# Output products of linear attention as 64-row tiles, the heads of either parity in a bank of their own, two chunks at once

## The chip, the cores and the metric

One core of one Trainium2 chip. Times are device microseconds of one execution, medians of several; a lower time is better. The engines are named as in the profile: PE is TensorE's matmul row, PEld its weight loads, DVE VectorE, ACT ScalarE, POOL GpSimd, SP the engine that issues most transfers.

## The reference

```python
# q, k, v: (batch 8, heads 8, seq 576, dim 64); all float32
kv  = einsum('bhsd,bhse->bhde', k, v)              # one 64x64 state per head
out = einsum('bhsd,bhde->bhse', q, kv)             # the output products: what the change is about
out = out / sqrt(mean(out**2, -1) + 1e-6) * g_norm
x   = out.transpose(0, 2, 1, 3).reshape(4608, 512)
xn  = x / sqrt(mean(x**2, -1) + 1e-6) * rms_g
y   = (silu(xn @ w_gate) * (xn @ w_val)) @ w_out   # 512 -> 1536 -> 512
```

## The kernel before

Everything is bfloat16 on TensorE, with float32 sums in PSUM. Of each batch's 576 tokens, 512 are worked on in a stage of their own (four chunks of 128 tokens); the 64 tokens left over of all eight batches make a ninth stage ("tail"). A stage has twelve units of gate and value products (`up`, eight matmuls of 512 columns each) and then four blocks of down products. While the units of batch n run, the attention of batch n+1 is slipped in between them: the state products of k and v, then the output products of a chunk after each of four units. Batches 0 and 1 are done by other code.

Two heads sit together in the 128 partitions of `qt`. Their states stand as two 64x64 blocks on the diagonal of a 128x128 block of `kv_all`, whose other two blocks are zero, so that one full-size product gives both heads, and half of its multiplications are with zeros.

```python
# four PSUM pools of two banks each (gate, value, down, attention)
outa_pool = pool("outa", 4)
gps_pool = pool("gps", 2, space=PS)
vps_pool = pool("vps", 2, space=PS)
ops_pool = pool("ops", 2, space=PS)
att_pool = pool("att", 2, space=PS)

# class Att (batches 2 to 7 and the tail)
def o_products(self, c, ps):
    for j in range(NS):                               # NS = 4 pairs of heads
        cols = ps[:, 2 * j : 2 * j + 2, :]
        if self.tail:
            ...                                       # 128-row, 64-column tiles, one per batch of two
        else:
            PE.matmul(
                cols, lhsT=self.qt[:, j, 128 * c : 128 * c + 128], rhs=kv_all[:, self.n, j, :],
                start=(j == 0), stop=(j == NS - 1),
            )

def o(self, c):
    ps = att_pool.tile([128, H, D], FP32, name="att_ps")
    self.o_products(c, ps)
    self.sq[c] = sq_pool.tile([128, 2, H, D], BF16, name="sq")
    SC.activation(out=self.sq[c][:, 0], in_=ps, func=ACT.Square)
    self.outa[c] = outa_pool.tile([128, H, D], BF16, name="outa")
    SC.copy(out=self.outa[c], in_=ps)

def sums(self, c):                                    # VectorE: the sums of squares of a chunk
    ...

# the schedule: what follows which unit of batch n
    kv0, os = (2, (4, 5, 7, 8)) if n == 1 else (0, (2, 3, 5, 6))
    if not a.tail:
        steps[kv0] += [lambda a=a: a.kv_products((0, 1))]
        steps[kv0 + 1] += [lambda a=a: a.kv_products((2, 3)), a.kv_copy]
    for c, u in enumerate(os):
        steps[u].append(lambda a=a, c=c: a.o(c))
        steps[u + 1].append(lambda a=a, c=c: a.sums(c))
    late = 2 * int(n == 1)
    steps[8 + late] += [a.head]
    steps[9 + late] += [a.guess, a.root]
    ...                                               # then scale and transpose each chunk
```

## Time and profile before

| | before |
|---|---|
| median (first three runs) | 324.66 us (324.35 to 336.14) |
| profiled run, span, granted clock | 324.46 us, 322.7 us, 1.0 |
| twelve units with attention of batches 3 to 7 | 22.73 us |
| twelve units of the last stage, nothing slipped in | 20.73 us |
| four down blocks | 10.36 us |

The page of the kernel before. In the upper part are busy time, share of the span and number of instructions; in the groups, count, then busy time and mean ns of one, then the idle time ahead of them and what ended it.

```profile
span 322.7 us, 5143 instructions
PE 316.0 (98%) x1925; PEld 156.5 (49%) x1925; DVE 181.5 (56%) x373; ACT 178.3 (55%) x318; POOL 20.3 (6%) x42
...
L352 ACT ACTIVATE sq<-att_ps 128x512 bf16<-128x512 f32 x28 | 16.7, 597 | 13.1 <-PE att_ps L343 8.7
L354 ACT CAST outa<-att_ps 128x512 bf16<-128x512 f32 x28 | 16.2, 579 | 0.0
L343 PEld LDWEIGHTS <-qt 128*128 128x128 bf16 x96 | 7.4, 98 | 5.7
L343 PE MATMUL att_ps<-kv_all,qt 128*128 128x128 bf16 x96 | 9.3, 219 | 0.0
```

PE has no idle time worth the name; no other engine passes 56%. The 96 output products look like 9.3 us of PE, but matmuls overlap in their pipeline and a duration of 219 ns is a latency. What a product costs is the distance from its start to the next start.

The stretches of stages, kernel before: busy time of each engine within each stretch, the number of instructions, the granted clock.

```profile
core 0: us, PE busy (x) PEld busy (x) DVE busy (x) ACT busy (x) POOL busy (x), PEclk, DMA share, GB/s
...
122.30:145.03 22.73, 22.73 (x133) 11.42 (x132) 15.65 (x32) 13.02 (x25) 0.00 (x0) 1.00 0.70 186
```

PE fills the whole stretch and the others have a third of it to spare, so what is slipped in between the units lengthens the stage by its PE time and by nothing else. Over the 20.73 us of the last stage it is 2.0 us: 20 state products and 16 output products of 128 columns at 56 ns.

The timeline of PE around two chunks, kernel before (start, time until the last of the merged instructions ends, what they are, how many):

```profile
160.82 1.03 PE L472 MATMUL v_ps<-xnt,wv_sb 128*128 128x512 bf16 x4
161.69 0.39 PE L343 MATMUL att_ps<-kv_all,qt 128*128 128x128 bf16 x4
161.91 1.03 PE L472 MATMUL g_ps<-xnt,wg_sb 128*128 128x512 bf16 x4
162.78 1.03 PE L472 MATMUL v_ps<-xnt,wv_sb 128*128 128x512 bf16 x4
163.64 0.39 PE L343 MATMUL att_ps<-kv_all,qt 128*128 128x128 bf16 x4
```

Four value products take 4 x 216 ns, 160.82 to 161.69. Four output products take 161.69 to 161.91: 0.22 us, 4 x 56 ns. Two chunks: 448 ns.

The kernel before holds smaller tiles already, and they show what going in and out of them costs. PE's timeline around the state products of batch 1 (64x64 tiles), and around the first chunk of the tail (128x64):

```profile
39.10 1.03 PE L472 MATMUL v_ps<-xnt,wv_sb 128*128 128x512 bf16 x4
40.06 1.32 PE L265 MATMUL att_ps<-vb,kb 64*64 64x64 bf16 x72
41.31 1.04 PE L516 MATMUL o_ps<-wo_sb,h_sb 128*128 128x512 bf16 x4
...
258.98 1.03 PE L472 MATMUL v_ps<-xnt,wv_sb 128*128 128x512 bf16 x4
259.94 0.41 PE L338 MATMUL att_ps<-kv_all,qt 128*64 128x128 bf16 x8
260.28 1.04 PE L472 MATMUL g_ps<-xnt,wg_sb 128*128 128x512 bf16 x4
```

From 258.98 to 259.94 is 0.96 us where 4 x 216 ns = 0.86 are due: the first tile comes 0.1 us late. Its eight products are four pairs that run side by side, 56 ns a pair, which would be 0.22 us; they take 0.34. So another 0.1 us is lost on the way out. PE counts as busy all the time, since the 379 ns of the matmul before cover the gap. What does show it is the weight loads: those of the same tiles have idle time ahead of them that is put down to "issue", that is, to nothing that the profile sees. From the view of that source line, kernel before:

```profile
L338 PEld LDWEIGHTS <-qt x32: 106/110/110, 259.9 to 268.3; 128*64 128x64 bf16 x32
...
its engine sat idle before it (us, times) until:
  issue: 1.7, 4
```

### The profile page before, as it was taken

Reading aid. Unit: us, or ns where it says so; the run is one execution under the profiler, and the core shown is the slowest. Engines: PE = TensorE matmul, PEld = TensorE weight load, DVE = VectorE, ACT = ScalarE, POOL = GpSimd, SP = SyncE. Lnnn points to the kernel's source line nnn. Section 1 sums busy time; section 2 is a strip of 40 time slices with the busy share of each in tenths; the row PEclk is TensorE's granted clock in tenths of the full one; section 3 lists DMA queues with packets and bytes.
Section 4 is the critical chain, followed back from the end, with each engine's and each line's share of the span. In section 5 each row is a group of like instructions: output and inputs, shape, how many; then the busy total and the mean of one; then the engine's idle time right before and its main releaser. Section 6 shows DMA issues by size and latency. Waiting matters only on the chain.

```text
span 322.7 us, 5143 instructions
## 1 busy us (share of the span) xinstructions
PE 316.0 (98%) x1925; PEld 156.5 (49%) x1925; DVE 181.5 (56%) x373; ACT 178.3 (55%) x318; POOL 20.3 (6%) x42
## 2 busy tenths in 40 slices
PE   8899999999999999999999999999999999999995
PEld 3575456554455445544554454445544444444443
DVE  4785767568438922793279417850696068703310
ACT  3576447666757475747664766576554355223321
POOL 1363251100000000000000000000000000000000
PEclk9999999999999999999999999999999999999999
DMA  7999999887379557924792378936102600240014
GB/s 277 355 351 386 377 374 293 214 265 176 65 195 295 132 143 163 328 54 114 187 328 56 73 202 222 315 55 169 43 2 49 182 31 1 48 147 4 0 35 98
DMA packets 74421, 54.87 MB, mean 170 GB/s; under 512 B 42264, under 2 KB 67100, under 8 KB 74396
## 3 DMA queue, kind: packets, MB, share of 16 engines
q1 hardware_dynamic: 74016, 53.88, 58.4%
q10 hardware_dynamic: 380, 0.66, 0.6%
q8 instruction: 15, 0.25, 0.3%
q14 instruction: 10, 0.08, 0.1%
HBM read 37.75 MB, written 9.44 MB: 146 GB/s over the span
## 4 chain that ended last, share of the span: by engine, by line
PE 92%; DMA 4%; DVE 2%; SPq 0%; ACT 0%; issue 0%; DVEq 0%
PE g_ps L472 28%; PE v_ps L472 28%; PE o_ps L516 27%; DMA st<-in_q_dram 3%; PE att_ps L272 2%; PE att_ps L343 2%; PE v_ps L516 1%; PE g_ps L516 1%; DVE xna L453 1%; DMA out_dram<-o_sb 1%; PE v_ps L489 1%; PE o_ps L489 1%; PE g_ps L489 0%; PE att_ps L338 0%; PE att_ps L285 0%; PE att_ps L265 0%
## 5 line engine op out<-in xcount | busy, mean ns | idle before, releaser
L478 DVE TENSOR_TENSOR h_sb<-silu,v_ps 128x512 bf16<-128x512 bf16 x104 | 71.0, 683 | 110.3 <-ACT silu L477 66.9
L472 PE MATMUL g_ps<-xnt,wg_sb 128*128 128x512 bf16 x416 | 106.8, 379 | 0.0
L472 PE MATMUL v_ps<-xnt,wv_sb 128*128 128x512 bf16 x416 | 106.7, 379 | 0.0
L477 ACT ACTIVATE silu<-g_ps 128x512 bf16<-128x512 f32 x104 | 62.5, 601 | 64.4 <-PE g_ps L472 53.7
L516 PE MATMUL o_ps<-wo_sb,h_sb 128*128 128x512 bf16 x396 | 87.4, 379 | 0.0
L472 PEld LDWEIGHTS <-wv_sb 128*128 128x128 bf16 x416 | 40.7, 98 | 49.1
L516 PEld LDWEIGHTS <-h_sb 128*128 128x128 bf16 x420 | 40.7, 98 | 47.7
L472 PEld LDWEIGHTS <-wg_sb 128*128 128x128 bf16 x416 | 38.7, 98 | 40.0 <-issue 0.4
L106 ACT COPY o_sb<-o_ps 128x512 f32<-128x512 f32 (+1 forms) x34 | 19.7, 580 | 38.0 <-PE o_ps L516 37.3
L361 DVE TENSOR_REDUCE ssq<-sq 128x16 f32<-128x1024 bf16 x28 | 34.1, 1219 | 1.0
L352 ACT ACTIVATE sq<-att_ps 128x512 bf16<-128x512 f32 x28 | 16.7, 597 | 13.1 <-PE att_ps L343 8.7
L106 ACT CAST vb<-st 128x512 bf16<-128x512 f32 (+2 forms) x33 | 18.9, 625 | 4.7 <-DMA st<-in_v_dram 4.7
L378 DVE TENSOR_TENSOR xna<-outa,s1y 128x512 bf16<-128x512 bf16 x28 | 17.9, 684 | 0.0
L354 ACT CAST outa<-att_ps 128x512 bf16<-128x512 f32 x28 | 16.2, 579 | 0.0
L106 ACT CAST qb<-st 128x1024 bf16<-128x1024 f32 (+1 forms) x15 | 14.2, 987 | 1.9 <-DMA st<-in_q_dram 1.9
L106 ACT CAST kb<-st 128x512 bf16<-128x512 f32 (+1 forms) x25 | 14.0, 619 | 0.0
L360 DVE TENSOR_TENSOR sq<-sq,gsq 128x512 bf16<-128x512 bf16 x28 | 11.7, 418 | 0.0
L343 PEld LDWEIGHTS <-qt 128*128 128x128 bf16 x96 | 7.4, 98 | 5.7
L343 PE MATMUL att_ps<-kv_all,qt 128*128 128x128 bf16 x96 | 9.3, 219 | 0.0
L272 PEld LDWEIGHTS <-kb 128*128 128x128 bf16 x120 | 7.7, 98 | 2.8
L617 PE MATMUL att_ps<-kv_all 128*128 128x512 bf16 (+1 forms) x21 | 7.6, 490 | 1.2 <-DVE sel L606 1.2
L272 PE MATMUL att_ps<-vb,kb 128*128 128x128 bf16 x120 | 8.7, 219 | 0.0
(141 smaller groups left out, 166.9 us busy)
## 6 DMA issues: line engine op xcount, KB each, us to landing
st<-in_q_dram SPq DMA_DIRECT2D x7, 1024.0 KB, 6.5
out_dram<-o_sb SPq DMA_DIRECT2D x14, 512.0 KB, 3.2
st<-in_k_dram SPq DMA_DIRECT2D x6, 1024.0 KB, 10.2
st<-in_v_dram SPq DMA_DIRECT2D x6, 1024.0 KB, 11.2
st<-in_moe_w_out_dram SPq DMA_DIRECT2D x6, 512.0 KB, 11.4
st<-in_moe_w_gate_dram SPq DMA_DIRECT2D x4, 512.0 KB, 9.4
st<-in_moe_w_val_dram SPq DMA_DIRECT2D x4, 512.0 KB, 9.8
st<-in_k_dram SPq DMA_DIRECT2D x4, 288.0 KB, 4.0
```

What stands on the lines that cost most here:

```text
L106: engine.copy(out=dst, in_=src)
L272: PE.matmul(ps, lhsT=bufs[b]["k"][:, t, hs, :], rhs=bufs[b]["v"][:, t, hs, :], start=(first and t == 0), stop=(last and t == T),)
L343: PE.matmul(cols, lhsT=self.qt[:, j, 128 * c : 128 * c + 128], rhs=kv_all[:, self.n, j, :], start=(j == 0), stop=(j == NS - 1),)
L352: SC.activation(out=self.sq[c][:, 0], in_=ps, func=ACT.Square)
L354: SC.copy(out=self.outa[c], in_=ps)
L360: DVE.tensor_tensor(out=sq[:, 1], in0=sq[:, 0], in1=gsq8, op=OP.mult)
L361: DVE.reduce_sum(out=self.ssq[:, c], in_=sq, axis=AX.X)
L378: DVE.tensor_tensor(out=self.xna[c], in0=self.outa[c], in1=self.alpha[:, c, :].to_broadcast([128, H, D]), op=OP.mult)
L472: PE.matmul(ps, lhsT=wt[:, s, j * 128 : (j + 1) * 128], rhs=x[:, s, :], start=(s == 0), stop=(s == NS - 1),)
L477: SC.activation(out=silu, in_=g_ps, func=ACT.Silu)
L478: DVE.tensor_tensor(out=self.h[:, j, :], in0=silu, in1=v_ps, op=OP.mult)
L516: PE.matmul(self.o_ps[c], lhsT=self.h[:, j, c * 128 : (c + 1) * 128], rhs=wo_sb[:, j, :], start=(j == 0), stop=(j == NF - 1),)
```

## The change

The intent: a head needs 64 rows of the array and 64 columns of its state, so the zero blocks can be left out. Each full-size product of 128 columns becomes two products of 64 rows and 64 columns that can run side by side, one in the upper half of the array (even heads), one in the lower (odd heads). Their outputs fall on the same 128 PSUM partitions, so either parity has a bank. As a chunk then fills half of two banks, two chunks are computed at once and share them; their evictions still follow two successive units.

```diff
-    outa_pool = pool("outa", 4)
+    outa_pool = pool("outa", 2)
@@ class Att
         def o(self, c):
             ps = att_pool.tile([128, H, D], FP32, name="att_ps")
             self.o_products(c, ps)
+            self.put_o(c, ((ps, slice(0, H)),))
+
+        def o_pair(self, i):
+            self.banks = [
+                att_pool.tile([128, 2, H // 2, D], FP32, name="att_ps") for _ in range(2)
+            ]
+            for c in range(2):
+                tokens = slice(128 * (2 * i + c), 128 * (2 * i + c) + 128)
+                for j in range(NS):
+                    for u in range(2):
+                        rows = slice(u * D, u * D + D)
+                        PE.matmul(
+                            self.banks[u][:, c, j, :], lhsT=self.qt[rows, j, tokens],
+                            rhs=kv_all[rows, self.n, j, rows],
+                            start=(c == 0 and j == 0), stop=(c == 1 and j == NS - 1),
+                        )
+
+        def put_pair(self, c):
+            self.put_o(c, [(self.banks[u][:, c % 2], slice(u, H, 2)) for u in range(2)])
+
+        def put_o(self, c, parts):
             self.sq[c] = sq_pool.tile([128, 2, H, D], BF16, name="sq")
-            SC.activation(out=self.sq[c][:, 0], in_=ps, func=ACT.Square)
-            self.outa[c] = outa_pool.tile([128, H, D], BF16, name="outa")
-            SC.copy(out=self.outa[c], in_=ps)
+            if c % 2 == 0:
+                self.outs = outa_pool.tile([128, 2, H, D], BF16, name="outa")
+            self.outa[c] = self.outs[:, c % 2]
+            for ps, hs in parts:
+                SC.activation(out=self.sq[c][:, 0, hs, :], in_=ps, func=ACT.Square)
+                SC.copy(out=self.outa[c][:, hs, :], in_=ps)
@@ the schedule
             for c, u in enumerate(os):
-                steps[u].append(lambda a=a, c=c: a.o(c))
+                if a.tail:
+                    steps[u].append(lambda a=a, c=c: a.o(c))
+                else:
+                    if c % 2 == 0:
+                        steps[u].append(lambda a=a, c=c: a.o_pair(c // 2))
+                    steps[u].append(lambda a=a, c=c: a.put_pair(c))
                 steps[u + 1].append(lambda a=a, c=c: a.sums(c))
```

(Batch 1's `o` takes its rows out of the same pair tile.)

More of the change, by code (lines that the diff above doesn't have):

```diff
@@ L433, in o @@
             self.o_products(c, ps)
-            self.outa[c] = outa_pool.tile([128, H, D], BF16, name="outa")
+            if c % 2 == 0:
+                self.outs = outa_pool.tile([128, 2, H, D], BF16, name="outa")
+            self.outa[c] = self.outs[:, c % 2]
             cast(engine, self.outa[c], ps)
@@ L977 @@
             for c, u in enumerate(os):
-                steps[u].append(lambda a=a, c=c: a.o(c))
+                if a.tail:
+                    steps[u].append(lambda a=a, c=c: a.o(c))
+                else:
+                    if c % 2 == 0:
+                        steps[u].append(lambda a=a, c=c: a.o_pair(c // 2))
+                    steps[u].append(lambda a=a, c=c: a.put_pair(c))
                 steps[u + 1].append(lambda a=a, c=c: a.sums(c))
```

## The prediction

> **What bounds the kernel now.** TensorE. The page gives it 98% of the 322.7 us span at granted clock 1.0; the chain of waits is 92% PE and runs from 56 to 316 us through products with no wait between them. In the steady stages (six batches, e.g. 155.56 to 178.28 us in the table of stretches) PE is busy 22.72 of 22.72 us, DVE 15.8, ACT 13.2. A gate-and-value stage alone takes 20.73 us (the last one). The other 2.0 us are 20 state products and 16 output products of 128 columns at 56 ns start to start. So only PE streaming time counts.
>
> **What goes.** The output products of batches 2 to 7: 96 matmuls 128x128 with 128 columns. In the raw starts four of them lengthen the distance between their neighbours from 216 to 440 ns: 224 ns a chunk, 448 ns per two chunks, 5.4 us in all 24 chunks. Half of that work multiplies the zero blocks of the state.
>
> **What comes.** Twelve groups of 16 matmuls: 64 rows, all 128 columns, 64 streamed columns, parities alternating between two row tiles and two banks. The Trainium skill (TensorEngine Tiling (Array Packing), Key Properties) says that tiles run in parallel but that changing the tiling mode drains the array. This trace shows both, in the 64x64 state products of batch 1: the two tiles start 3 ns apart and a pair follows every 32 ns; but the first starts 309 ns after the last full-size matmul instead of 216, the second pair comes after 52 ns, and after the last pair the next full-size matmul comes only 125 ns later and its successor 227 instead of 216. The 128x64 products of the tail show the same (309 in, 152 out; 655 ns in place of 440). Even the 64x128 products of the constant rows pay 95 ns in and 95 out.
>
> Estimate for a group, from these durations: 93 (drain in) + 52 + 6x32 + 3 + 125 + 10 = about 475 ns, against 448 now. The halved stream (about 195 ns) is eaten by two mode changes (about 220 ns). Net +0.03 us a group, +0.3 us in twelve.
>
> ACT: four instructions of 256 columns per chunk in place of two of 512. The 512-column ones follow each other at 0.50 us; the 64x256 cast takes 0.37 against 0.58. I estimate 1.15 to 1.3 us a chunk instead of 1.08: about 0.1 to 0.2 us x 24 = 2.5 to 5 us more ACT busy. Silu then comes up to 0.3 us later in some units; both PSUM pairs are double-buffered and a unit lasts 1.73 us, so PE should not wait. Off the path. The two attention banks are free again (about 1 us into the unit after next) well before the second group, three units later. The pair tile of the rows has the same bytes as before.
>
> **Predicted: 325.0 us, 8 in 10 between 322.8 and 327.0.** Faster by over 2%: 0.01; within 2%: 0.97; slower by over 2%: 0.02.
>
> **What would show it.** Steady stages 22.7 to 22.85 us; PE still without waits; the last value matmul before a group to the first gate matmul after it about 690 ns; the row tiles 3 to 4 ns apart, pairs about 32 ns; first tile about 93 ns late.
>
> **What would make it wrong.** If a row-only mode change drains less, up to 2.3 us are won (322.4). If the two row tiles do not run together, because both write all 128 PSUM partitions or because 128-column weight loads serialise (25 ns each in the small sums products), a group takes 0.58 to 0.67 us: 1.6 to 2.7 us lost. If ACT's longer evictions delay silu past the double buffer, PE gaps appear in the units just after a group.

## The result, and the profile after

The change took 325.19 us (median of 6, 324.39 to 325.40), the kernel before 324.67 us. The ratio is 1.0016, with a 95% interval of 1.0002 to 1.003. A ratio here is the mean time of one kernel's runs over that of the other's of the same rounds, so it is not quite the ratio of the medians. Executions over 1.5% slower than the fastest of the same kernel are left out of the means. Kernels are compared only within the same rounds.

The page after, and (last two lines) its groups with shapes kept apart:

```profile
span 323.5 us, 5354 instructions
PE 313.6 (97%) x1986; PEld 153.8 (48%) x2021; DVE 181.6 (56%) x373; ACT 179.9 (56%) x366; POOL 20.3 (6%) x42
...
L378 ACT ACTIVATE sq<-att_ps 128x256 bf16<-128x256 f32 (+1 forms) x52 | 22.5, 433 | 10.0 <-PE att_ps L363 7.5
L379 ACT CAST outa<-att_ps 128x256 bf16<-128x256 f32 (+1 forms) x52 | 22.0, 423 | 0.0
...
L363 PE MATMUL att_ps<-kv_all,qt 64*128 64x64 bf16 x192 | 4.9, 191 | 0.0
L363 PEld LDWEIGHTS <-qt 64*128 64x128 bf16 x192 | 3.5, 95 | 5.1 <-issue 5.1
```

The busy time of the output products has nearly halved, 9.3 to 4.9 us, as has that of their weight loads. A reader of busy time alone would book 4.4 us of gain. The stretches of the stages say otherwise:

```profile
core 0: us, PE busy (x) PEld busy (x) DVE busy (x) ACT busy (x) POOL busy (x), PEclk, DMA share, GB/s
...
123.03:145.76 22.73, 22.57 (x147) 10.91 (x149) 15.43 (x32) 13.33 (x33) 0.00 (x0) 1.00 0.66 185
```

The stage takes 22.73 us as before. PE's timeline around one group of two chunks shows why:

```profile
161.55 1.03 PE L499 MATMUL v_ps<-xnt,wv_sb 128*128 128x512 bf16 x4
162.51 0.41 PE L363 MATMUL att_ps<-kv_all,qt 64*128 64x64 bf16 x16
162.85 1.04 PE L499 MATMUL g_ps<-xnt,wg_sb 128*128 128x512 bf16 x4
```

161.55 to 162.51 is 0.96 us instead of 0.86, and the sixteen products with the way out take 0.34 us. In the raw starts, from the last value product before to the first gate product after it are 651 ns. The two row tiles start 3 to 4 ns apart, pairs follow at 29 ns (39 for the second); the first comes 311 ns after the value product instead of 216, the next gate product 122 ns after the last one, and the one after that 227 ns later instead of 216. So a group costs 651 - 216 + 11 = 446 ns, where two chunks of before cost 448. The 5.1 us of "issue" ahead of the weight loads are the twelve ways in, 0.42 us each, where two weight loads of a unit have 216 - 98 = 118 ns between them.

Where then do the profiled runs differ, 322.7 to 323.5 us? First, ahead of batch 0's first gate product, which nothing edited touches: it starts at 17.15 us instead of 16.60, since a transfer of q took longer. From the chain of waits, before and after:

```profile
7.37 5.50 DMA st<-in_q_dram
```

```profile
7.43 6.00 DMA st<-in_q_dram
```

Second, ahead of the third batch. PE's timeline at the end of batch 1's down products, before and after:

```profile
87.82 1.46 PE L516 MATMUL o_ps<-wo_sb,h_sb 128*128 128x512 bf16 x6
89.22 0.59 PE L472 MATMUL g_ps<-xnt,wg_sb 128*128 128x512 bf16 x2
```

```profile
88.35 1.46 PE L543 MATMUL o_ps<-wo_sb,h_sb 128*128 128x512 bf16 x6
89.94 0.59 PE L499 MATMUL g_ps<-xnt,wg_sb 128*128 128x512 bf16 x2
```

Six down products of 216 ns are 1.30 us; the next gate product should start at 89.12 and at 89.65. It starts 0.1 us late before (its rows of x come off the end of VectorE's chain) and 0.29 us late after. That stage's down part takes 10.65 us instead of 10.46. Every later stage is the same to 0.01 us, and the earlier ones from the first gate product on to 0.02 us (batch 0's units take 24.72 and 24.70).

### The profile page after: what moved, and what is told of

It is laid out like the page before. It is cut to its first block, busy times and chain, and to the rows that moved or that the text cites. A ratio compares the mean times of both kernels' runs of the same rounds, so it can differ in the third digit from the quotient of the medians.

```text
span 323.5 us, 5354 instructions
## 1 busy us (share of the span) xinstructions
PE 313.6 (97%) x1986; PEld 153.8 (48%) x2021; DVE 181.6 (56%) x373; ACT 179.9 (56%) x366; POOL 20.3 (6%) x42
## 4 chain that ended last, share of the span: by engine, by line
PE 90%; DMA 4%; DVE 3%; issue 1%; SPq 0%; ACT 0%; DVEq 0%
PE g_ps L499 27%; PE v_ps L499 27%; PE o_ps L543 26%; DMA st<-in_q_dram 3%; PE att_ps L272 2%; PE att_ps L363 1%; PE v_ps L543 1%; PE g_ps L543 1%; DVE xna L480 1%; DMA out_dram<-o_sb 1%; PE o_ps L516 1%; PE g_ps L516 0%; PE att_ps L338 0%; PE att_ps L265 0%; PE att_ps L285 0%
## 5 line engine op out<-in xcount | busy, mean ns | idle before, releaser
L499 PE MATMUL g_ps<-xnt,wg_sb 128*128 128x512 bf16 x399 | 104.9, 379 | 1.1 <-ACT wg_sb L201 0.2
L378 ACT ACTIVATE sq<-att_ps 128x256 bf16<-128x256 f32 (+1 forms) x52 | 22.5, 433 | 10.0 <-PE att_ps L363 7.5
L379 ACT CAST outa<-att_ps 128x256 bf16<-128x256 f32 (+1 forms) x52 | 22.0, 423 | 0.0
L644 PE MATMUL att_ps<-kv_all 128*128 128x512 bf16 (+1 forms) x19 | 6.9, 497 | 1.2 <-DVE sel L633 1.2
L108 DVE CAST kb<-st 128x576 bf16<-128x576 f32 (+1 forms) x12 | 5.9, 516 | 1.8 <-DMA st<-in_k_dram 1.7
L201 ACT ACTIVATE wg_sb<-st,rowscale 128x256 bf16<-128x256 f32 (+1 forms) x10 | 5.5, 585 | 0.8 <-DMA st<-in_moe_w_gate_dram 0.8
```

Source lines behind the costliest of these rows:

```text
L378: SC.activation(out=self.sq[c][:, 0, hs, :], in_=ps, func=ACT.Square)
L379: SC.copy(out=self.outa[c][:, hs, :], in_=ps)
L499: PE.matmul(ps, lhsT=wt[:, s, j * 128 : (j + 1) * 128], rhs=x[:, s, :], start=(s == 0), stop=(s == NS - 1),)
L644: PE.matmul(ps[:, 0:w], lhsT=warm_sb[:, 0:128], rhs=warm_sb[:, 0:w], start=True, stop=True, skip_group_check=True)
```

## The experiments

Theory A: a group of tiles costs a fixed 0.21 us for two changes of the tiling mode, whatever it holds, and 29 ns for each pair of tiles that runs side by side; eight pairs are just where that breaks even with 56 ns for each full-size product. Rival R reads the same 446 ns otherwise: sixteen products at 28 ns, one after another, with no concurrency and no drain. It would give the same total for the change. The first four runs tell the two apart. All kernels below gave correct results. "Group" is the time that it adds between its neighbours, from the raw starts.

### One group of four chunks

```diff
+ self.quad = [p.tile([128, 2, H // 2, D], FP32, name=nm)
+     for p, nm in ((att_pool, "att_ps"), (att_pool, "att_ps"), (ops_pool, "o_ps"), (ops_pool, "o_ps"))]
+ for c in range(T): ...   # all four chunks; bank 2 * (c // 2) + u
@@ schedule
- if a.tail:                 # single full-size chunks
+ if a.tail or n == 1:
```

> Batches 3 to 7 only: all four chunks in one group of 32 row-tile products (two more banks borrowed from the down products), batch 2 as before the change. Theory A (two mode changes cost about 214 ns a group, whatever its length, and a pair of row tiles streams in 29 ns): one group per batch is 214 + 16x29 = 678 ns where the kernel before spends 896 ns; steady stages 22.5 us instead of 22.73, the kernel 1.1 us faster than before (ratio 0.9966). Rival R (no concurrency and no drain, simply 28 ns for each of the products): 32x28 = 896 ns, stages stay 22.73 us, ratio 1.000. In both, the gap before the third batch's first gate product is as in before (about 0.1 us).

Measured: 323.36 us against 324.38, ratio 0.9968 (0.9956 to 0.998). Stages 22.52 us; a group adds 680 ns. A holds to 2 ns; R is off by 216 ns. One group on PE's timeline (four banks, hence two lines; its first product starts 311 ns after the last value product):

```profile
161.87 0.41 PE L381 MATMUL att_ps<-kv_all,qt 64*128 64x64 bf16 x16
162.11 0.40 PE L381 MATMUL o_ps<-kv_all,qt 64*128 64x64 bf16 x16
162.44 1.04 PE L517 MATMUL g_ps<-xnt,wg_sb 128*128 128x512 bf16 x4
```

### One chunk at a time

```diff
- for c in range(2):         # o_pair: sixteen products, twelve times
+ # o_one(c): eight products, twenty-four times; both banks half filled
```

> The row tiles kept, but one chunk at a time (8 products a group, 24 groups). Theory A: 214 + 4x29 = 330 ns a chunk against 224 before, stages 23.15 us instead of 22.73, 2.5 us slower than before (ratio 1.008). Rival R (28 ns per product and nothing else): 224 ns a chunk, ratio 1.000.

Measured: 327.37 us, ratio 1.0101 (1.0083 to 1.012). Stages 23.15 to 23.16 us, a group adds 330 ns. Again A. The total is some 0.5 us more than the stages account for; the trace has part of it ahead of the first gate product (17.6 us), where traces differ anyway (below). One group:

```profile
163.15 1.03 PE L498 MATMUL v_ps<-xnt,wv_sb 128*128 128x512 bf16 x4
164.11 0.29 PE L362 MATMUL att_ps<-kv_all,qt 64*128 64x64 bf16 x8
164.33 1.04 PE L498 MATMUL g_ps<-xnt,wg_sb 128*128 128x512 bf16 x4
```

Together the three sizes lie on a line: 330, 446 and 680 ns for 4, 8 and 16 pairs are 214 ns + 29 ns a pair, to 2 ns.

### The parities one after the other

```diff
- for c in range(2):
-     for j in range(NS):
-         for u in range(2):
+ for u in range(2):
+     for c in range(2):
+         for j in range(NS):
```

> As the change, but a group runs the eight products of the even heads, then the eight of the odd ones, so that neighbours are always in the same row tile. Theory A: no two products run together, 16x28 + about 190 to 214 = 640 to 660 ns a group against 446, 2.4 us slower than the change (ratio to before about 1.009). Rival R: as the change, ratio 1.0016.

Measured: 326.44 us, ratio 1.0066 (1.0054 to 1.0079). Stages 22.99 us, a group adds 578 ns, which is 0.13 us more than the change's 446. So concurrency is real and is worth at least this much, and R falls. But the size was missed: with no overlap at all, 214 + 16 x 29 = 678 ns were due. The starts of one group, in us (from the trace's records), show two trains of eight, each with one step of 38 or 39 ns and then 29 ns, the second of which sets off while the first has three products to go:

```
162.599  .638  .667  .696  .725         .755         .784         .813
                                 .734         .772         .801         .830  .860  .889  .918  .948
```

The records do not name the tile; that the second train is the odd parity is inferred from its step and from the two 200 ns durations (190 for the rest) that the first product of a train has. The semaphores in the same records bear it out, in all twelve groups alike: the first and the sixth start (.599 and .734) wait for a semaphore, as the first product of either parity does in the change, and the eleventh (.813) and the last start signal one. In the program it is the eighth and the sixteenth product that signal, so three products of the odd parity started before the last of the even one. PE thus started products for the idle row tile ahead of earlier ones for the busy tile, by the recorded starts; the ends are modelled and show no order.

### The mode change alone

```diff
 # kernel before, ahead of every second chunk
+ PE.matmul(ps[:, 0, 0:1], lhsT=self.qt[0:D, 0, 0:128], rhs=kv_all[0:D, self.n, 0, 0:1],
+           start=True, stop=True, skip_group_check=True)      # overwritten by the chunk
```

> The kernel before with one 64-row product of a single column (its result is overwritten) put ahead of every second chunk of batches 2 to 7, 12 in all: the mode change by itself. Theory A: about 95 ns in, 95 out and 14 of catching up, 0.2 us each, 2.4 us in all (ratio 1.0075). Rival R: 12x28 ns = 0.3 us (ratio 1.001).

Measured: 327.06 us, ratio 1.0082 (1.0069 to 1.0095), 2.7 us. Stages 23.16 us, 0.43 more for two of them. The first output product starts 418 ns after the value product instead of 216, and the second one 67 ns later instead of 56: 213 ns for one product of one column. PE's timeline there:

```profile
162.18 1.03 PE L477 MATMUL v_ps<-xnt,wv_sb 128*128 128x512 bf16 x4
163.13 0.17 PE L351 MATMUL att_ps<-kv_all,qt 64*128 64x1 bf16 x1
163.24 0.40 PE L343 MATMUL att_ps<-kv_all,qt 128*128 128x128 bf16 x4
```

This is the fixed term of the line, measured almost by itself: the lone product's own step is in it (96 ns in, 106 to the next start, 11 of catching up), so that it meets the line's 214 to 1 ns is in part luck.

### Full-size products, two chunks at once

```diff
 # kernel before (the tail as it was)
+ if c % 2 == 0:
+     self.two = [att_pool.tile([128, H, D], FP32, name="att_ps") for _ in range(2)]
+     for i in range(2):
+         self.o_products(c + i, self.two[i])
+ ps = self.two[c % 2]
```

> The kernel before, with its own full-size products and its own evictions, but the products of two chunks at once: no mode change, no row tiles. It isolates the 0.19 us by which the change lengthens the wait ahead of the third batch (down stage of batch 1: 10.65 us against 10.46). Theory L (the second chunk's products now stand ahead of the next unit, so VectorE's chain of gate products, sums and scales in that stage ends 0.2 us later): the distance ahead of the third batch's first gate product is about 510 ns, as in the change, the down stage of batch 1 10.65 us, the kernel 0.2 us slower than before (ratio 1.0006). Rival E (the four shorter evictions of ScalarE are what comes later): 312 ns, 10.46 us, ratio 1.000. Steady stages 22.73 us in both.

Measured: 325.04 us, ratio 1.0031 (1.0013 to 1.0049). Down part of batch 1: 10.64 us, the distance ahead of the third batch 499 ns. Theory L holds and E falls: the lengthened wait comes from moving the second chunk's products ahead of the next unit, neither from tiles nor from evictions. PE at the end of that stage:

```profile
87.42 1.46 PE L523 MATMUL o_ps<-wo_sb,h_sb 128*128 128x512 bf16 x6
89.00 0.59 PE L479 MATMUL g_ps<-xnt,wg_sb 128*128 128x512 bf16 x2
```

The records show the path too. From the gate product after the first pair of chunks on, all of VectorE's chain in batch 1's stage runs 0.22 us later; the last scaling of batch 2's rows starts 27.70 us into the stage in the kernel before, 27.92 in the change and 27.92 here. The ratio is larger than the 0.2 us of the trace; one of its six executions took 326.68 us, and what that one was is open.

### The change without its first batch

```diff
- if a.tail:
+ if a.tail or n == 1:       # batch 2 as before the change
```

> The change, but batch 2 (whose chain ends on the critical path) keeps the products of before. Both theories of the 0.19 us: down stage of batch 1 back at 10.46 us. Theory A: ten groups at 2 ns less than before, steady stages 22.73 us, ratio 1.000. If instead the change's remaining loss (0.3 us, ahead of the first gate product, where nothing was edited) comes with the larger program, it stays: ratio 1.001, with the first gate product at 17.1 us or later.

Measured: 324.63 us against 324.38, ratio 1.0013 (0.9999 to 1.0028). Down part of batch 1: 10.44 us; stages 22.72 to 22.75 us. The 0.2 us of the wait is gone (the last scaling starts at 27.72 us), the ratio scarcely moves. That left 0.3 us for which the larger program was still a candidate, and asked for a control.

### The change again, and the kernel before against itself

Both unedited.

> The change itself once more, unedited, for a second trace and for the size of the loss on the chip of the other runs. Steady stages 22.73 us, down stage of batch 1 10.65 us, ratio 1.0006 by what the trace places after the first gate product, 1.0016 if the loss ahead of it returns.

> The kernel before against itself: what a ratio is worth without any change, and a second trace of the stretch ahead of the first gate product (16.6 us in the first trace). If that stretch differs only by chance, the first gate product lies anywhere in the 16.3 to 17.6 us of the other traces and the ratio is within 0.999 to 1.001.

Measured: the change 324.78 us, ratio 1.0014 (1.0001 to 1.0027), with 10.67 us for the down part of batch 1. The kernel before against itself: 324.92 us against 324.21, ratio 1.0013 (0.9998 to 1.0027). A ratio of 1.001 can therefore come of no change at all in this set-up, outside the band that I had expected, and the change's 1.0016 is not told apart from it. The first gate product of this second trace of before started at 17.41 us, later than in either trace of the change (17.15 and 16.75): the stretch ahead of it differs by chance, and no run points to the larger program.

What the times can't resolve, the traces can, if the first 41 us are left out. From batch 0's first down product to that of the last stage the two traces of the kernel before take 266.95 and 266.91 us, those of the change 267.14 and 267.16, `full_pair` 267.13 and `pairs_but_first` 266.95. In these traces, then, the change costs 0.2 us, and the lengthened wait is all of it.

### Fewer mode changes elsewhere

If a mode change costs 0.21 us and a pair of tiles half of a full-size product, the rule is: few groups, long ones. `fewest_switches` applies it to `four_chunks`, in two more places.

```diff
 # state products of batches 2 to 7: 128-row, 64-column tiles, one group of 40
- PE.matmul(ps, lhsT=bufs[b]["k"][:, t, hs, :], rhs=bufs[b]["v"][:, t, hs, :], ...)
+ for u in range(2):
+     rows = slice(u * D, u * D + D)
+     PE.matmul(ps[rows, rows], lhsT=bufs[b]["k"][:, t, 2 * j + u, :], rhs=bufs[b]["v"][:, t, 2 * j + u, :], ...)
- steps[kv0] += [lambda a=a: a.kv_products((0, 1))]
- steps[kv0 + 1] += [lambda a=a: a.kv_products((2, 3)), a.kv_copy]
+ steps[kv0 + 1] += [lambda a=a: a.kv_products((0, 1, 2, 3)), a.kv_copy]
 # the tail: all four chunks after one unit, banks as in four_chunks
```

> four_chunks and two more uses of the same finding: the state products of batches 2 to 7 as 128-row, 64-column tiles, all four head pairs in one group, and the four tail chunks in one group. Theory A with the 32 ns per pair of tiles that the batch-1 state products show: 214 + 20x32 = 854 ns against 1120 for each of six batches (1.6 us less in all; stages of 22.25 us), tail stage 214 + 16x56 = 1110 against 1796 ns (0.7 us less, 21.83 us), output products 1.1 us less as measured. 3.4 us faster than before, ratio 0.9895. If column tiles of 64 columns stream at 56 ns a pair like those of the tail, the state products take 1334 ns, stages 22.73 us, ratio 0.998.

Measured: 322.19 us, ratio 0.9936 (0.9922 to 0.995). A state group adds 858 ns (854 expected), the tail's group 1120 (1110); stages 22.25 to 22.26 us, tail stage 21.84. But batch 2's stage, which works on the attention of batch 3, took 23.08 us: its fourth chunk of `qt` was asked for with the first and had not landed. From the waits of that stretch:

```profile
PEld L382 <- DMA qt<-qb: 0.8, 1, 0.8
PE o_ps L382 <- DMA qt<-qb: 0.6, 1, 0.6
```

The ratio missed the expected 0.9895 for the most part by this wait: from batch 0's first down product to that of the last stage the trace takes 264.43 us, 2.5 less than the 266.95 of the kernel before, and with the 0.82 us of the wait that makes 3.3 of the 3.4 expected.

So I put that one group a unit later:

```diff
- kv0, os = (2, (4, 5, 7, 8)) if n == 1 else (0, (2, 3, 5, 6))
+ kv0, os = (2, (4, 5, 7, 8)) if n == 1 else (0, (3, 4, 6, 7)) if n == 2 else (0, (2, 3, 5, 6))
```

> fewest_switches with the group of batch 3 one unit later (its fourth chunk of q had not landed: 0.8 us of PE wait, that stage 23.08 us). Theory A: that stage 22.25 us like the other four, no PE wait for qt; 3.0 us faster than before (ratio 0.991).

Measured: 322.16 us, ratio 0.9935 (0.9922 to 0.9948). A miss: the wait for `qt` went, but a wait of another kind came and the stage took 23.24 us. PE's timeline at its end:

```profile
109.54 1.03 PE L526 MATMUL g_ps<-xnt,wg_sb 128*128 128x512 bf16 x4
111.39 0.38 PE L526 MATMUL v_ps<-xnt,wv_sb 128*128 128x512 bf16 x1 [0.83 <-DVE h_sb L532]
```

And VectorE's timeline just before it:

```profile
107.79 0.42 DVE L412 TENSOR_TENSOR sq<-sq,gsq 128x512 bf16<-128x512 bf16 x1
108.24 1.22 DVE L413 TENSOR_REDUCE ssq<-sq 128x16 f32<-128x1024 bf16 x1
109.50 0.18 DVE L417 TENSOR_SCALAR u<-ssq 128x32 f32<-128x32 f32 x1
...
110.55 0.19 DVE L230 SCALAR_TENSOR_TENSOR sz<-sm,u 128x32 f32<-128x32 f32 x1
110.66 0.68 DVE L532 TENSOR_TENSOR h_sb<-silu,v_ps 128x512 bf16<-128x512 bf16 x1
```

The last sums and the head of the chain of scales now fall between the same two gate products. VectorE reaches the second at 110.66, and until it ends at 111.34 the value bank that PE wants is held. The chain has to move along with the group:

```diff
- late = 2 * int(n == 1)
+ late = {1: 2, 2: 1}.get(n, 0)
```

> fewest_switches_2 with batch 3's chain of scales put off by one unit as well (head after unit 9, root after unit 10, all scales after unit 11): in fewest_switches_2 VectorE stood with sums and head between two gate products and held a value bank, 1.0 us of PE wait at the end of that stage (23.24 us). If that is the cause, the stage is 22.25 us like the other four, with no new wait ahead of the next stage, 1.0 us less than fewest_switches_2: about 321.2 us, ratio 0.9905. If the wait only moves again, to the start of the next stage, the sum of that stage and its down stage stays above 33.0 us (32.6 expected) and the ratio 0.9935.

Measured: 321.27 us against 324.38, ratio 0.9907 (0.9891 to 0.9924), the best of all. That stage takes 22.26 us. A quarter of a microsecond came back at the start of the next (its down part 10.62 us instead of 10.36): 32.88 us for the two, between the 32.6 expected and the 33.0 of the other outcome.

### Left open

Both parities in one bank per chunk, which would have undone the "bank of their own" and kept two evictions a chunk, was built but not run: a static race check reports that two row tiles would write the same bank without an order between them. What the own banks buy was therefore not measured.

## Why the prediction was right

It said 325.0 us, 322.8 to 327.0, and that the halved stream would be eaten by two mode changes. The time was 325.19 and that is the mechanism. Point by point:

- PE alone bounds the stages: right. ScalarE was busy 0.3 us longer per stage (13.02 to 13.33) and the stages did not change.
- A group of 475 ns, in terms 93 in, 52 + 6x32 + 3 of stream, 125 + 10 out: measured 446, in terms 95, 39 + 6x29 + 4 = 217, 122 + 11. The ways in and out were read rightly off the 64x64 products; the stream was mis-sized by 30 ns, because I took the pace of those smaller tiles (52 ns, then 32) for the 64-row ones (39, then 29). So the groups cost at most 0.02 us less than before in all, where 0.3 us more was predicted.
- "Even the 64x128 products of the constant rows pay 95 ns in and 95 out": the fixed cost was confirmed by itself, 213 ns for a lone product, in `lone_switch`.
- If the row tiles did not run together a group would take 0.58 to 0.67 us: `parity_turns`, where they mostly don't, took 0.58. That this lies in the range is in part luck: with no overlap at all, the line gives 0.68.
- 1.15 to 1.3 us of ScalarE a chunk: about 1.2 in the timeline. The sum of 2.5 to 5 us more was too high; per stage it was at most 0.31 us, over the six stages 1.7 us.
- "PE still without waits": wrong in one place. I followed the evictions from ScalarE to the banks, but not what moving the second chunk's products ahead does to VectorE, whose chain ends batch 1's stage on the critical path. There 0.19 us were lost, which `full_pair` shows without any tile, and `pairs_but_first` shows gone.
- The sum came out near because one small error (+0.3) stood about where the missed wait (+0.2) belonged; and the control shows that a difference of this size, 0.1%, is not resolved by the times at all. What the traces show is that groups are neutral to 2 ns each, and that one wait grew by 0.2 us.

## What to carry to other kernels

Halving the work of a matmul by tiling is worth (full-size time minus tile-pair time) x pairs, minus a fixed price per excursion from full-size work; here 27 ns a pair against 214 ns, so eight pairs (two chunks) win nothing, sixteen win 0.22 us, and the price is hidden from busy time: look for distances between starts and for idle "issue" time ahead of the tile's weight loads. Having found a fixed price, lengthen the groups and cut their number, then check each moved piece for what now arrives too early (a transfer) or too late (a chain on another engine). Before explaining a tenth of a per cent, time the kernel against itself.

## What the Trainium skill lacked or had wrong

- TensorEngine Tiling (Array Packing), Key Properties, says that a change of tiling mode drains the engine, and gives no price. Here an excursion into a 64-row mode costs 214 ns by a line through three group sizes, and 213 ns for a single product: 95 ns on the way in, the rest a slower second pair and the way out; so the "up to 2x" of its Theoretical Speedup table needs more than eight pairs of 64-column products in a row before it gains anything.
- TensorE: Matmul & The Clock Gate, The mechanism (in Part 3), says that matmuls start and end strictly in program order, without reordering. In `parity_turns` sixteen products in two runs of eight took 348 ns from first to last start instead of 15 x 29 = 435, with a second train of starts among the first: products for the idle row tile went ahead of earlier ones. That is by the recorded starts; the order of the ends is not shown, as the ends are modelled. The start distance of about 4 ns between tiles, in the same section's diagram and in Measured speedup vs the span model after it, agrees (3 to 4 ns).
- TensorE: Matmul & The Clock Gate, Wait — 56ns, not 53.3ns? (in Part 1), gives about 25 ns as the least start-to-start distance of matmuls. With tiles it holds within a tile, not between products: those of two tiles start 3 to 4 ns apart, and a pair of them comes every 29 ns for two 64-row products of 64 columns, every 32 ns for two 64-column ones (570 ns for the last 18 steps of a group in `fewest_switches`).
- No page says how the drain of a mode change looks in a profile: PE stays busy through it, and it appears as 0.42 us of "issue" ahead of the first weight load of a group (5.1 us in twelve), where two weight loads of a unit have 0.12 us between them (216 - 98 ns).
